# Turning packed probabilities by VectorE blocks and DMAs in place of TensorE transposes

## The chip, the cores and the metric

The kernel runs on one NeuronCore of a Trainium2 chip. Its five engines follow their own instruction queues: TensorE (PE, with its weight loads shown as PEld), VectorE (DVE), ScalarE (ACT), GpSimd (POOL) and SyncE (SP), which here issues nearly all DMAs. The metric is the device time of one execution in microseconds (us), lower is better. The kernel before took 697.37 us, the median of 3 runs (696.98 to 698.82).

## The reference

The inputs are q, k and v of shape 4 x 8 x 768 x 64 (batch, heads, positions, head size) in fp32 and two weight matrices, 512 x 2048 and 2048 x 512. A causal attention with a window of 128 keys and 4 sink keys is followed by a two-layer network:

```
scores = scale * q @ k.T                       # scale = 1/8
keep = (key < 4) | (0 <= query - key < 128)
a = softmax(where(keep, scores, -1e9))
x = (a @ v) with heads side by side            # 3072 tokens x 512
h = x @ w_in
out = max(0.01 * h, h) @ w_out                 # 3072 x 512
```

## The kernel before

The 3072 tokens are cut into 8 **units** of 384 queries (three blocks of 128), two units to a batch element: an even unit holds the first half of a sequence, an odd one the second. In a unit the 8 heads go in 4 **pairs**. Each unit also has 16 steps of the two-layer network (below: **MLP steps**). In an MLP step 12 matmuls form `h` (L584, fp32 split into a high and a low part, so three matmuls per product), ScalarE and VectorE form `g` (L598, L605), ScalarE rounds it to `gh` (L606), GpSimd forms the rest `gl` (L607), and one MLP step later 9 matmuls add into the output `o` (L633); the last three of the nine need `gl`.

The program interleaves the attention of unit u+1 with the MLP of unit u. The order on TensorE is fixed by this interleaving (`manual_schedule` for PE alone): a generator of attention steps is advanced by a table of due steps, eight steps per pair. Work that has to come some score tiles later is put into a list with a lag: `later(LAGT, ...)` with LAGT = 2, and `later(LAGP, ...)` with LAGP = 5 score tiles for the values of a packed pair. The order on the other engines comes from a scheduler.

From the third unit on ("packed" units, 24 pairs, 48 heads) the window of a query block spans the previous and the own key block, and the two halves of the window are stored in one 128 x 128 square: a position of the square holds the own key where it is allowed and the previous block's key elsewhere (`copy_predicated`, L518). So a head has three squares of 128 queries x 128 keys and 4 sink columns, held in `pk` (128 x 396), made by `soft` (L322, L324) and scaled by 1/sum at L525 to L527. The product with the values needs keys on partitions, so each square is turned by a TensorE transpose into a PSUM bank (`turn_packed`, L364), three per head; for the second head of a pair a fourth transpose turns the sinks (`sk`, L366). VectorE then multiplies the turned squares by two triangle masks `low` and `upp` (L383) and writes them side by side into `pt` in SBUF, previous part and own part of each query block; in an even unit the first block needs no mask and is copied by ScalarE (L378). `values` (L406) multiplies `pt` with the values into `acc` (L412 for sinks, L416 for keys), then ScalarE and VectorE split the result into `xh` and `xl` (L432, L433). `pt` has one buffer.

The heads' inputs `qkraw` (three buffers), the pair's values `v` and the pair's sink values `svr` are loaded by SyncE; `svr` lives in the one `rb` buffer.

Of the kernel before, what the change touches and what calls it, by code (L numbers as in the profile page):

```python
# [9 lines left out]
F32 = mybir.dt.float32  # L10
# [10 lines left out]
P = 128  # L21
# [15 lines left out]
NVB = (3, 4)  # L37
SPARE = W3 + NSK
SCALE = 1.0 / D ** 0.5
MASKED = 1.0e38  # L40
# [107 lines left out]
def fast_path(ctx, tc, cpool, qp, qk, vu, vs, vx, vt, wq, out, ident, lims, wz, negm, wmin, wmax):  # L148
# [4 lines left out]
    mpool = ctx.enter_context(tc.tile_pool(name="mpool", bufs=2))  # L153
    iopool = ctx.enter_context(tc.tile_pool(name="iopool", bufs=2))
    psum = ctx.enter_context(tc.tile_pool(name="psum", bufs=1, space=PSUM))
    lim_raw, lim_lo, rest, masks = build_masks(tc, cpool, xpool, lims)
# [89 lines left out]

    def load_sinks(u, pair):
        if native(u):
            sv = apool.tile([SKR, TU], F32, tag="sv", name=f"sv{u}_{pair}")
            if u:  # L250
                nc.sync.dma_start(out=sv[0:T * SKN, :], in_=vx[pair])
            else:
                nc.sync.dma_start(out=sv[0:SKN, :], in_=vs[pair])
            svs[u, pair] = sv
            return
        raw = xpool.tile([SKR, TU], F32, tag="rb", name=f"svr{u}_{pair}", bufs=1)[:, 0:P]
        nc.sync.dma_start(out=raw, in_=vt[u // 2, pair])
        svs[u, pair] = raw

# [39 lines left out]
    def turn_bank(u, name):  # L299
        tags = ("t", "o2") if u == 0 else ("t",)  # L300
        seq["t"] += 1
        return bank(tags[(seq["t"] - 1) % len(tags)], name)
# [56 lines left out]

    def turn_packed(u, pair, o, w, state):  # L360
        half = u % 2
        tp = turn_bank(u, f"t{u}_{pair}_{o}")
        for j in range(T):
            nc.tensor.transpose(out=tp[:, j * P:(j + 1) * P], in_=w[:, j, NSK:], identity=ident)  # L364
        if o:
            nc.tensor.transpose(out=tp[:, TU:], in_=state["sk"].rearrange("p r j h s -> p (r j h s)"), identity=ident)  # L366
            st = xpool.tile([P, P + TU], F32R, tag="r", name=f"st{u}_{pair}")[:, 0:TU]
            state["st"] = st
            nc.vector.tensor_tensor(out=st.rearrange("p (j q) -> p j q", j=T),
                                    in0=tp[:, TU:].rearrange("p (o q) -> p o q", o=1).broadcast_to([P, T, P]),  # L370
                                    in1=late[0][4].rearrange("p (j o) -> p j o", o=1).broadcast_to([P, T, P]),
                                    op=ALU.mult)
        pt = state["pt"][:, o]
        src = tp[:, 0:TU].rearrange("p (j q) -> p j q", j=T)
        if half:
            dst = pt
        else:
            nc.scalar.copy(out=pt[:, 0:P], in_=tp[:, 0:P])  # L378
            dst, src = pt[:, P:5 * P], src[:, 1:T]
        dst = dst.rearrange("p (j t q) -> p t j q", t=2, q=P)  # L380
        n = T - 1 + half
        for t, mask in enumerate(late[0][2:4]):
            nc.vector.tensor_tensor(out=dst[:, t], in0=src,  # L383
                                    in1=mask.rearrange("p (o q) -> p o q", o=1).broadcast_to([P, n, P]), op=ALU.mult)

# [20 lines left out]
    def values(u, pair, state):  # L406
# [7 lines left out]
        for kb, (po, qo, m) in enumerate(parts):  # L414
            for o in range(2):
                nc.tensor.matmul(acc[o * D:(o + 1) * D, qo:qo + m],  # L416
                                 lhsT=vv[:, kb * P + o * D:kb * P + (o + 1) * D],
                                 rhs=state["pt"][:, o, po:po + m], start=kb == 0 and not packed,
                                 stop=packed and kb == len(parts) - 1, skip_group_check=True)
# [22 lines left out]
    def attend(u, pair, pend):  # L442
# [63 lines left out]
        else:  # L506
            for o in range(2):
                h = 2 * pair + o
                sp = split_head(u, h)
                fetch(o)  # L510
                (split_sinks if o else load_sinks)(u, pair)
                w = apool.tile([P, 2 * W3], F32, tag="pk", name=f"pk{u}_{h}", bufs=3)
                w = w[:, 0:T * W1].rearrange("p (j k) -> p j k", j=T)
                sm = apool.tile([P, T], F32, tag="sm", name=f"sm{u}_{h}")
                for j in range(T):
# [8 lines left out]
                    if j == T - 1:  # L524
# [9 lines left out]
                                                op=ALU.subtract)  # L534
                        later(LAGT, lambda o=o, w=w: pt_then(turn_packed, u, pair, o, w, state))
                    yield
        last = u == 0 and pair == NPAIR - 1
        if native(u):
            later(LAGT if last else LAGG, lambda: gather(u, pair, state))
        later(LAGT if last else LAGV if native(u) else LAGP, lambda: values(u, pair, state),  # L540
              "next" if not native(u) else "scores" if u else None)

    def attention_stream():
# [6 lines left out]
        for u in range(NU):  # L550
            for pair in range(NPAIR):
                for _ in attend(u, pair, pend):
                    if pend and pend[0][0] <= count[0] and pend[0][2] == "scores":
                        pend.pop(0)[1]()
                    yield
                    while pend and pend[0][0] <= count[0]:
                        _, f, join = pend.pop(0)
                        f()
                        if not (join == "next" and pend and pend[0][0] <= count[0]):
                            yield  # L560
# [340 lines left out]
```

## Time and profile before

| what | value |
|---|---|
| median of 3 runs | 697.37 us |
| the profiled execution, first to last instruction | 697.4 us |
| TensorE busy | 684.6 us, 98% |
| VectorE busy | 451.0 us, 65% |
| ScalarE, GpSimd busy | 319.4 us, 317.7 us |
| DMA: mean rate | 107 GB/s |
| granted TensorE clock | 0.999 |

Busy time on TensorE counts each matmul until its modelled end, and matmuls overlap, so the share alone does not say how much of the time a removed matmul gives back; start times of neighbouring matmuls do. The page gives no time outside the span of the profiled execution; the span and the median of the runs agree within 0.1 us.

### The profile page before, as it was taken

The numbers are of one execution on the slowest core, as the hardware profiler recorded it, in microseconds if no ns is written. First come the engines' busy times: TensorE is split into PE (matmuls) and PEld (weight loads), VectorE is DVE, ScalarE is ACT, GpSimd is POOL, SyncE is SP. The second block draws the span as 40 slices with busy tenths as digits, with TensorE's granted clock in tenths as the row PEclk, the third lists the DMA queues.
The fourth block names the chain that finished last, engine by engine and source line by source line (L and its number), as shares of the span: only waits on it lengthen the run. The fifth ranks groups of instructions, "written<-read, shape, count | busy, mean of one in ns | idle before, by whom it ended". The sixth has DMA issues, their size and how long they took to land.

```text
span 697.4 us, 11523 instructions
## 1 busy us (share of the span) xinstructions
PE 684.6 (98%) x3938; PEld 596.6 (86%) x3938; DVE 451.0 (65%) x1192; ACT 319.4 (46%) x836; POOL 317.7 (46%) x436
## 2 busy tenths in 40 slices
PE   8999999999999999999999999999999999999996
PEld 5578888898888988888898888898888889899995
DVE  5799999655566665565566565566566666377772
ACT  4867675444444444444444444444444444222221
POOL 3767797544543543443453354344344344112221
PEclk9999999999999999999999999999999999999999
DMA  6657666311213111222113221121221311068761
GB/s 223 214 170 230 212 208 209 128 57 44 73 45 118 47 43 62 61 85 70 59 57 102 70 59 46 62 92 43 69 74 45 118 63 46 1 196 278 257 190 49
DMA packets 30656, 74.55 MB, mean 107 GB/s; under 512 B 3584, under 2 KB 9472, under 8 KB 30592
## 3 DMA queue, kind: packets, MB, share of 16 engines
q1 hardware_dynamic: 30448, 73.63, 32.8%
q8 instruction: 32, 0.52, 0.3%
q14 instruction: 32, 0.26, 0.1%
q10 hardware_dynamic: 144, 0.13, 0.1%
HBM read 67.45 MB, written 6.29 MB: 106 GB/s over the span
## 4 chain that ended last, share of the span: by engine, by line
PE 92%; DVE 2%; DMA 2%; POOL 2%; ACT 1%; issue 1%; SPq 0%; DVEq 0%; POOLq 0%; ACTq 0%
PE h L584 37%; PE o L633 37%; PE acc L416 5%; PE s L315 5%; PE t L364 3%; PE s L310 2%; PE t L351 1%; DMA qkn<-in_qp 1%; DMA qkraw<-in_qk 1%; PE acc L422 0%; PE acc L412 0%; POOL gl L607 0%; ACT pk L324 0%; PE t L366 0%; DMA svr<-in_vt 0%
## 5 line engine op out<-in xcount | busy, mean ns | idle before, releaser
L607 POOL TENSOR_TENSOR gl<-g,gh 128x384 fp32r<-128x384 f32 x121 | 125.0, 1033 | 261.9 <-ACT gh L606 228.4
L584 PE MATMUL h<-xh,wih 128*128 128x384 f32 x512 | 179.1, 350 | 1.1 <-DVE g L605 1.1
L584 PE MATMUL h<-xl,wih 128*128 128x384 f32 x512 | 172.7, 337 | 0.1
L584 PE MATMUL h<-xh,wil 128*128 128x384 f32 x512 | 172.6, 337 | 0.0
L633 PE MATMUL o<-woh,gh 128*128 128x512 f32 (+1 forms) x400 | 153.8, 386 | 0.0
L633 PE MATMUL o<-wol,gh 128*128 128x512 f32 (+1 forms) x400 | 153.2, 386 | 0.0
L324 ACT ACTIVATE pk<-pk,negm 128x132 f32<-128x132 f32 (+1 forms) x192 | 81.6, 425 | 97.6 <-DVE negm L322 97.4
L633 PE MATMUL o<-woh,gl 128*128 128x512 f32 (+1 forms) x400 | 114.7, 388 | 0.7 <-POOL gl L607 0.7
L598 ACT ACTIVATE g<-h 128x384 f32<-128x384 f32 x127 | 62.0, 488 | 112.8 <-PE h L584 96.1
L584 PEld LDWEIGHTS h<-xh,wih 128*128 128x128 f32 x512 | 96.3, 188 | 5.7 <-issue 2.9
L584 PEld LDWEIGHTS h<-xl,wih 128*128 128x128 f32 x512 | 96.6, 189 | 1.6 <-POOL xl L430 0.5
L584 PEld LDWEIGHTS h<-xh,wil 128*128 128x128 f32 x512 | 96.1, 188 | 0.0
L606 ACT CAST gh<-g 128x384 fp32r<-128x384 f32 x128 | 65.7, 513 | 64.3 <-DVE g L605 64.1
L605 DVE TENSOR_TENSOR g<-h,g 128x384 f32<-128x384 f32 x127 | 69.9, 550 | 31.2 <-ACT g L598 30.8
L633 PEld LDWEIGHTS o<-woh,gl 128*128 128x128 f32 x400 | 73.5, 188 | 17.3 <-POOL gl L607 1.6
L633 PEld LDWEIGHTS o<-woh,gh 128*128 128x128 f32 x400 | 75.2, 188 | 10.6
L633 PEld LDWEIGHTS o<-wol,gh 128*128 128x128 f32 x400 | 75.1, 188 | 10.7
L276 POOL TENSOR_TENSOR qksp<-qkraw,qksp 64x396 fp32r<-64x396 f32 (+1 forms) x48 | 56.5, 1177 | 43.4 <-issue 27.5
L518 DVE COPY_PREDICATED s<-tri,s 128x128 f32<-128x128 int8 x120 | 34.9, 291 | 52.0 <-PE s L315 50.5
L315 PEld LDWEIGHTS s<-qksp 128*128 128x128 f32 x288 | 53.4, 188 | 7.9
L275 ACT CAST qksp<-qkraw 128x780 fp32r<-128x780 f32 (+1 forms) x48 | 43.2, 900 | 30.4 <-PE s L315 27.3
L315 PE MATMUL s<-qksp 128*128 128x260 f32 (+1 forms) x288 | 56.3, 277 | 0.0
(123 smaller groups left out, 861.7 us busy)
## 6 DMA issues: line engine op xcount, KB each, us to landing
craw<-in_wq SPq DMA_DIRECT2D x26, 512.0 KB, 4.6
qkraw<-in_qk SPq DMA_DIRECT2D x24, 454.0 KB, 3.2
qkraw<-in_qk SPq DMA_DIRECT2D x24, 390.0 KB, 3.0
wiraw<-in_wq SPq DMA_DIRECT2D x16, 512.0 KB, 3.8
woraw<-in_wq SPq DMA_DIRECT2D x16, 512.0 KB, 3.7
out<-ob SPq DMA_DIRECT2D x23, 256.0 KB, 2.1
v<-in_vu SPq DMA_DIRECT2D x16, 256.0 KB, 2.6
v<-in_vu SPq DMA_DIRECT2D x16, 192.0 KB, 2.5
```

Source lines behind the costliest of these rows:

```text
L275: nc.scalar.copy(out=sp[:, 0:TU + n], in_=raw[:, 0:TU + n])
L276: nc.gpsimd.tensor_tensor(out=sp[D:P, TU:TU + n], in0=raw[D:P, TU:TU + n], in1=sp[D:P, TU:TU + n].bitcast(F32), op=ALU.subtract)
L315: nc.tensor.matmul(pss[0][:, 0:kn], lhsT=sp[:, off + j * P:off + (j + 1) * P], rhs=sp[:, TU + k0:TU + k0 + kn], start=c == 0, stop=c == 1)
L324: nc.scalar.activation(out=w, in_=w, func=AF.Exp, scale=-1.0, bias=neg, accum_out=sm)
L416: nc.tensor.matmul(acc[o * D:(o + 1) * D, qo:qo + m], lhsT=vv[:, kb * P + o * D:kb * P + (o + 1) * D], rhs=state["pt"][:, o, po:po + m], s ...
L518: nc.vector.copy_predicated(out=ps[:, W1:W3], mask=late[0][1], data=ps[:, 0:P])
L584: nc.tensor.matmul(ph[:, 0:TU], lhsT=w[:, cs], rhs=x, start=cc == 0 and c == 0, stop=cc == NCC - 1 and c == 2)
L598: nc.scalar.mul(g, ph[:, 0:TU], 0.01)
L605: anchor[0] = nc.vector.tensor_tensor(out=g, in0=ph[:, 0:TU], in1=g, op=ALU.max)
L606: nc.scalar.copy(out=gh, in_=g)
L607: (nc.vector if u and fc == NFC - 1 else nc.gpsimd).tensor_tensor(out=gl, in0=g, in1=gh.bitcast(F32), op=ALU.subtract)
L633: nc.tensor.matmul(acc, lhsT=(gl if c == 2 else gh)[:, t * P:(t + 1) * P], rhs=(wl if c == 1 else wh)[:, cols], start=f == 0 and c == 0, s ...
```

## The change

In packed units the three TensorE transposes of each head go. In their place `turn_blocks` does this for each head: VectorE transposes all 32 x 32 blocks of the three squares in one instruction (`pk` to `kt`, 128 x 384); one DMA writes `kt` to a DRAM buffer; four DMAs (one for each group of 32 keys) read it back into `pt`, so that the blocks land where a full transpose would have them. The contiguous runs of a read are 96 fp32 numbers (384 bytes). The masking becomes `mask_blocks`: two multiplications from SBUF to SBUF, `pt` by `low` into the second half of `pt` and `pt` by `upp` in place. The columns of `pt` now stand as group of 32 queries, then block, then query, so the matmuls of `values` read their moving operand as runs of 32 columns (`masked_keys`). The sinks' transpose stays on TensorE (`turn_sinks`). `svr` is loaded into the tail of the `pk` tile, and `kt` takes the one `rb` buffer. The first head of a pair is turned at lag 2 and masked at lag 3; the second is turned at lag 0 and masked at lag 2.

```
-        raw = xpool.tile([SKR, TU], F32, tag="rb", name=f"svr{u}_{pair}", bufs=1)[:, 0:P]
-        nc.sync.dma_start(out=raw, in_=vt[u // 2, pair])
-        svs[u, pair] = raw
+        nc.sync.dma_start(out=spare, in_=vt[u // 2, pair])
+        svs[u, pair] = spare
...
-    def turn_packed(u, pair, o, w, state):
...
+    def turn_blocks(u, pair, o, w, state):
+        kt = xpool.tile([P, TU], F32, tag="rb", name=f"kt{u}_{pair}_{o}", bufs=1)
+        nc.vector.transpose(kt.rearrange("p (b j x) -> p b j x", b=NSQ, x=SQ),
+                            w[:, :, NSK:].rearrange("p j (b x) -> p b j x", b=NSQ))
+        far = dpool.tile([P, NSQ, T * SQ], F32, tag="kt", name=f"kd{u}_{pair}_{o}", bufs=2)
+        nc.sync.dma_start(out=far.rearrange("p b x -> p (b x)"), in_=kt)
+        for b in range(NSQ):
+            nc.sync.dma_start(out=state["pt"][b * SQ:(b + 1) * SQ, o, 0:TU].rearrange("c (a x) -> c a x", a=NSQ),
+                              in_=far[:, b].rearrange("(a c) x -> c a x", a=NSQ))
...
+    def mask_blocks(u, o, state):
+        j0 = 1 - u % 2
+        n = T - j0
+        cur, prv = (state["pt"][:, o, i * TU:(i + 1) * TU].rearrange("p (a j x) -> p a j x", a=NSQ, j=T)[:, :, j0:]
+                    for i in range(2))
+        for dst, mask in ((prv, late[0][2]), (cur, late[0][3])):
+            nc.vector.tensor_tensor(out=dst, in0=cur, in1=mask.rearrange("p (a o x) -> p a o x", a=NSQ, o=1)
+                                    .broadcast_to([P, NSQ, n, SQ]), op=ALU.mult)
+
+    def masked_keys(state, o, j0, n):
+        cur = state["pt"][:, o]
+        first = (j0 * SQ, TU + SQ) if j0 >= 0 else (TU, 0)
+        return bass.AP(cur.tensor, cur.offset + first[0],
+                       [cur.ap[0], [first[1], n], [T * SQ, NSQ], [1, SQ]])
...
-                                 rhs=state["pt"][:, o, po:po + m], start=kb == 0 and not packed,
+                                 rhs=masked_keys(state, o, qo // P - (0 if kb or not half else 1), m // P)
+                                 if packed else state["pt"][:, o, po:po + m], start=kb == 0 and not packed,
...
+                w = apool.tile([P, T * W1 + P], F32, tag="pk", name=f"pk{u}_{h}", bufs=3)
...
+                    load_sinks(u, pair, w[:, T * W1:])
...
-                        later(LAGT, lambda o=o, w=w: pt_then(turn_packed, u, pair, o, w, state))
+                        later(0 if o else LAGT, lambda o=o, w=w: pt_then(turn_blocks, u, pair, o, w, state), "quiet")
+                        if o:
+                            later(LAGT, lambda: turn_sinks(u, pair, state))
+                        later(LAGT if o else LAGT + 1, lambda o=o: mask_blocks(u, o, state), "quiet")
```

On VectorE, in the second pair of the sixth unit, the rows from the masks of the pair's first head to the next scaling of a head stood so before:

```order
L268 TENSOR_TENSOR sv_2_4672<-svr_2_4572,sv_2_4672 32x128
L383 TENSOR_TENSOR pt_1_4517<-t_1_0_4518,low 128x3x128
L383 TENSOR_TENSOR pt_1_4517<-t_1_0_4518,upp 128x3x128
L433 TENSOR_TENSOR xl_0_4514<-acc_0_4503,xh_0_4513 128x384
L605 TENSOR_TENSOR g_2_4527<-h_2_4493,g_2_4527 128x384
L518 COPY_PREDICATED s_3_2_4543<-tri,s_3_2_4543 128x128
L322 ISA pk_3_4457,negm<-s_3_2_4543,pm_676 128x132
L322 ISA negm 128x1
L525 TENSOR_SCALAR sm_3_4458<-sm_3_4458 128x3
```

and stand so now (`kt` is the block transpose, `xl_0` belongs to the values of the pair before, `g_1` and `g_2` to two MLP steps that follow each other):

```order
L364 STREAM_TRANSPOSE kt_1_0_4607<-pk_2_4428 128x384
L623 TENSOR_TENSOR g_1_4563<-h_1_4544,g_1_4563 128x384
L270 TENSOR_TENSOR sv_2_4760<-pk_4_4663,sv_2_4760 32x128
L445 TENSOR_TENSOR xl_0_4593<-acc_0_4582,xh_0_4592 128x384
L533 COPY_PREDICATED s_3_2_4615<-tri,s_3_2_4615 128x128
L324 ISA pk_3_4533,negm<-s_3_2_4615,pm_678 128x132
L324 ISA negm 128x1
L623 TENSOR_TENSOR g_2_4629<-h_2_4596,g_2_4629 128x384
L388 TENSOR_TENSOR pt_1_4606<-pt_1_4606,low 128x384
L540 TENSOR_SCALAR sm_3_4537<-sm_3_4537 128x3
L388 TENSOR_TENSOR pt_1_4606<-pt_1_4606,upp 128x384
```

The masks moved from ahead of `xl_0` to behind `g_2`, the next MLP step's `g`, and the block transpose stands one MLP step ahead of them.

On SyncE, for the same pair, the queue held three loads and no store of probabilities before:

```order
L244 DMA qkraw_4_4452<-in_qk 128x908
L244 DMA qkraw_5_4570<-in_qk 128x908
L257 DMA svr_2_4572<-in_vt 128x128
L234 DMA v_1_4127<-in_vu 128x512
L244 DMA qkraw_6_4670<-in_qk 128x908
```

and holds these now (`kd` is the DRAM buffer):

```order
L259 DMA pk_4_4663<-in_vt 128x128
L367 DMA kd_1_0_4609<-kt_1_0_4607 128x384
L237 DMA v_2_4424<-in_vu 128x512
L369 DMA pt_1_4606<-kd_1_0_4609 32x4x96 x4
L247 DMA qkraw_0_4980<-in_qk 128x780
L367 DMA kd_1_1_4649<-kt_1_1_4647 128x384
L369 DMA pt_1_4606<-kd_1_1_4649 32x4x96 x4
```

Between two loads of heads there are now one write and four reads, in order behind each other; the loads `qkraw` and `v` stand between them.

## Rows read from the trace of the kernel before

**Rows 1.** Page, busy us of each engine, share of the span, instructions.
```profile
PE 684.6 (98%) x3938; PEld 596.6 (86%) x3938; DVE 451.0 (65%) x1192; ACT 319.4 (46%) x836; POOL 317.7 (46%) x436
```
**Rows 2.** Busy time by stretches (stretch, its length, each engine's busy us).
```profile
107.00:190.00 83.00, 80.92 (x462) 71.29 (x461) 54.07 (x146) 39.64 (x109) 44.50 (x54) 1.00 0.31 101
...
358.00:441.00 83.00, 83.00 (x479) 73.67 (x478) 52.35 (x145) 37.77 (x98) 36.63 (x47) 1.00 0.22 66
```
**Rows 3.** Page, the chain that ended last, by engine and by line.
```profile
PE 92%; DVE 2%; DMA 2%; POOL 2%; ACT 1%; issue 1%; SPq 0%; DVEq 0%; POOLq 0%; ACTq 0%
PE h L584 37%; PE o L633 37%; PE acc L416 5%; PE s L315 5%; PE t L364 3%; PE s L310 2%; PE t L351 1%; DMA qkn<-in_qp 1%; DMA qkraw<-in_qk 1%; PE acc L422 0%; PE acc L412 0%; POOL gl L607 0%; ACT pk L324 0%; PE t L366 0%; DMA svr<-in_vt 0%
```
**Rows 4.** Groups by shape, transposes: busy us, mean ns | idle before.
```profile
L364 PE MATMUL t<-ident,pk 128*128 128x128 f32 x144 | 24.8, 281 | 0.0
```
**Rows 5.** Timeline of PE, an even unit (start us, us, engine, instruction).
```profile
136.34 1.30 PE L416 MATMUL acc<-pt,v 128*64 128x256 f32 x12
137.57 0.55 PE L364 MATMUL t<-ident,pk 128*128 128x128 f32 x3
137.88 0.48 PE L633 MATMUL o<-woh,gh 128*128 128x512 f32 x1
138.19 0.39 PE L633 MATMUL o<-wol,gh 128*128 128x512 f32 x1
138.42 0.39 PE L633 MATMUL o<-woh,gh 128*128 128x512 f32 x1
...
147.72 0.49 PE L364 MATMUL t<-ident,pk 128*128 128x128 f32 x3
148.04 0.27 PE L366 MATMUL t<-ident,sk 128*128 128x128 f32 x1
```
**Rows 6.** Timeline of PE, values of an odd unit.
```profile
387.23 1.52 PE L416 MATMUL acc<-pt,v 128*64 128x128 f32 x16
```
**Rows 7.** Groups by shape on DVE: busy us, mean ns | idle before.
```profile
L383 DVE TENSOR_TENSOR pt<-t,low 128x384 f32<-128x384 f32 x24 | 13.3, 553 | 16.9 <-PE t L364 16.9
L383 DVE TENSOR_TENSOR pt<-t,low 128x256 f32<-128x256 f32 x24 | 10.0, 416 | 1.3 <-ACT pt L378 1.3
...
L607 DVE TENSOR_TENSOR gl<-g,gh 128x384 fp32r<-128x384 f32 x7 | 3.9, 557 | 3.5 <-ACT gh L606 3.5
```
**Rows 8.** Lines L527 and L525: duration ns min/median/max, first and last start.
```profile
L527 DVE TENSOR_TENSOR pk<-pk,sm x48: 560/1182/1390, 109.8 to 600.0; 128x396 f32<-128x396 f32 x48
...
L525 DVE TENSOR_SCALAR sm<-sm x48: 157/763/1054, 108.0 to 599.5; 128x3 f32<-128x3 f32 x48
```
**Rows 9.** DMA issues: count, KB each, median us to landing.
```profile
out<-ob SPq DMA_DIRECT2D x23, 256.0 KB, 2.1
...
svr<-in_vt SPq DMA_DIRECT2D x24, 64.0 KB, 1.8
...
sv<-in_vs SPq DMA_DIRECT2D x4, 48.0 KB, 4.0
```
**Rows 10.** Timeline of SP's queue, three DMAs issued in a row.
```profile
380.64 1.52 SPq L648 DMA_DIRECT2D out<-ob  x3
```
**Rows 11.** Timeline of all engines, from one MLP step's `h` to the use of `gl`.
```profile
333.46 0.47 ACT L598 ACTIVATE g<-h 128x384 f32<-128x384 f32 x1
...
333.99 0.55 DVE L605 TENSOR_TENSOR g<-h,g 128x384 f32<-128x384 f32 x1
...
334.56 0.51 ACT L606 CAST gh<-g 128x384 fp32r<-128x384 f32 x1 [0.63 <-DVE g L605]
...
334.94 0.34 PE L584 MATMUL h<-xh,wih 128*128 128x384 f32 x1
...
335.12 0.34 PE L584 MATMUL h<-xl,wih 128*128 128x384 f32 x1
...
335.15 1.01 POOL L607 TENSOR_TENSOR gl<-g,gh 128x384 fp32r<-128x384 f32 x1 [0.46 <-PE s L315]
...
338.89 0.86 PE L633 MATMUL o<-woh,gl 128*128 128x512 f32 x3
```

More of the change, by code (lines that the diff above doesn't have):

```diff
@@ L38 @@
 SPARE = W3 + NSK
+SQ = 32
+NSQ = P // SQ
 SCALE = 1.0 / D ** 0.5
@@ L154, in fast_path @@
     iopool = ctx.enter_context(tc.tile_pool(name="iopool", bufs=2))
+    dpool = ctx.enter_context(tc.tile_pool(name="dpool", bufs=1, space=bass.MemoryType.DRAM))
     psum = ctx.enter_context(tc.tile_pool(name="psum", bufs=1, space=PSUM))
@@ L245, in load_head, with load_sinks @@
         raws[u, h] = raw
-    def load_sinks(u, pair):
+    def load_sinks(u, pair, spare=None):
         if native(u):
@@ L358, in turn_native @@
             split_sinks(u, pair)
-    def turn_packed(u, pair, o, w, state):
[L361 to L384, printed above, removed]
@@ new lines, in turn_sinks @@
+    def turn_sinks(u, pair, state):
+        tp = turn_bank(u, f"t{u}_{pair}")
+        nc.tensor.transpose(out=tp[:, 0:P], in_=state["sk"].rearrange("p r j h s -> p (r j h s)"), identity=ident)
+        st = xpool.tile([P, P + TU], F32R, tag="r", name=f"st{u}_{pair}")[:, 0:TU]
+        state["st"] = st
+        nc.vector.tensor_tensor(out=st.rearrange("p (j q) -> p j q", j=T),
+                                in0=tp[:, 0:P].rearrange("p (o q) -> p o q", o=1).broadcast_to([P, T, P]),
+                                in1=late[0][4].rearrange("p (j o) -> p j o", o=1).broadcast_to([P, T, P]),
+                                op=ALU.mult)
@@ L510, in attend @@
                 fetch(o)
-                (split_sinks if o else load_sinks)(u, pair)
-                w = apool.tile([P, 2 * W3], F32, tag="pk", name=f"pk{u}_{h}", bufs=3)
+                w = apool.tile([P, T * W1 + P], F32, tag="pk", name=f"pk{u}_{h}", bufs=3)
+                if o:
+                    split_sinks(u, pair)
+                else:
+                    load_sinks(u, pair, w[:, T * W1:])
                 w = w[:, 0:T * W1].rearrange("p (j k) -> p j k", j=T)
@@ L534, in attend @@
                                                 op=ALU.subtract)
-                        later(LAGT, lambda o=o, w=w: pt_then(turn_packed, u, pair, o, w, state))
+                        later(0 if o else LAGT, lambda o=o, w=w: pt_then(turn_blocks, u, pair, o, w, state), "quiet")
+                        if o:
+                            later(LAGT, lambda: turn_sinks(u, pair, state))
+                        later(LAGT if o else LAGT + 1, lambda o=o: mask_blocks(u, o, state), "quiet")
                     yield
@@ L540, in attend @@
         later(LAGT if last else LAGV if native(u) else LAGP, lambda: values(u, pair, state),
-              "next" if not native(u) else "scores" if u else None)
+              "scores" if u and native(u) else None)
     def attention_stream():
@@ L558, in attention_stream @@
                         f()
-                        if not (join == "next" and pend and pend[0][0] <= count[0]):
+                        if join != "quiet":
                             yield
```

## The prediction

> **What bounds the kernel now.** I read the page's busy line first, then stretches of one unit each, then the chain of waits, then start times on TensorE. The reader is to see that TensorE is busy 98% of the span [rows 1] and, in a middle unit, all of it: 83.00 of 83.00 us [rows 2]; no other engine reaches two thirds. The chain that ended last runs through TensorE for 92% of the span, and the transposes that go have 3% of it [rows 3]. So in the stretch this change touches (some 110 to 600 us, from the first and last start in rows 8) TensorE has no slack to lose, and what leaves its queue comes off the span, unless a wait appears in its place. The profiled execution (697.4 us) and the median (697.37) agree, so no correction is made between them.
>
> **What is removed.** 48 heads times 3 transposes are 144 matmuls. Their group is busy 24.8 us [rows 4], but that counts each run of three to its modelled end, 0.49 to 0.55 us. Starts tell what they occupy: three transposes start at 137.57, and the next matmul at 137.88, 0.31 us later; at 147.72 the next starts at 148.04, 0.32 us later [rows 5]. 48 x 0.32 = 15.4 us. After the first run the next interval is 0.31 (137.88 to 138.19) where 0.23 is usual (138.19 to 138.42), so up to 0.08 more could go, 48 x 0.08 = 3.8 us; but it may belong to any change between small and large matmuls, and one stays, so I count none of it. Ends of this term: 15.4 and 24.8; I take 15.4, since starts and not ends decide when the next matmul goes. The sinks' transpose stays and changes nothing. ScalarE loses the copy of an even unit's first block; it is off the chain [rows 3], so nothing.
>
> **What is added on TensorE.** Nothing in number: `values` has the same matmuls and columns, so no gain is possible. But the moving operand is now read in runs of 32 columns. No row shows such a read. The lower bound is no cost; the upper I set at twice the time: an even pair's 12 matmuls take 1.30 us [rows 5], an odd pair's 16 take 1.52 [rows 6], so 12 x 1.30 + 12 x 1.52 = 33.8 us. I take zero: matmuls here keep the pace of their columns, and a run is still 32 numbers side by side. Rival three keeps the other end.
>
> **What is added on VectorE.** 48 block transposes of 128 x 384. Not shown before; the nearest row of equal width from SBUF to SBUF is the `gl` that VectorE forms, 0.557 us, and the nearest that is slow is the scaling of a head, 128 x 396, with a median of 1.182 us [rows 7, 8]; a 256-column mask bounds it from below at 0.416. I take 0.56: 27 us over the kernel. The masks stay 96 instructions of the same widths (0.553 and 0.416 from PSUM), but now have two SBUF sources. Price between 0.557, the quick row, and 1.182, the slow one, for 384 columns. The scaling takes 0.560 at best and 1.390 at worst for the same shape, and an addition on 3 numbers 0.157 to 1.054 [rows 8]: some VectorE instructions wait about one GpSimd instruction (1.01 us, rows 11) when the two meet. I take half of the way, 0.3 us more for each mask, 29 us. VectorE then has 451 + 27 + 29 = 507 us of about 683, 74%. Per pair of a middle unit it is idle (83.00 - 52.35) / 4 = 7.7 us [rows 2] and gets 2 x 0.56 + 4 x 0.3 = 2.3 us more (4.8 at the dear end, 2 x 1.18 + 4 x 0.62). Cover is there in sum; what matters is the queue behind. Behind masks and transpose waits `g`, behind it `gh`, `gl`, and TensorE's last three `o` matmuls. That chain has `gl` ready at 335.15 + 1.01 = 336.16 and used at 338.89 [rows 11]: 2.7 us of slack per MLP step. The second head's transpose (0.56) and the first head's two masks (2 x 0.86 in place of 2 x 0.55) add 1.2 us ahead of one `g`: hidden.
> The Trainium skill has a rule for this (SBUF — State Buffer, "SBUF: two separate sides"): VectorE and GpSimd share one port pair as an exclusive lock, which a VectorE instruction with two SBUF inputs and a GpSimd instruction that reads SBUF take in turn, each for its whole length. It agrees with the spread of rows 8 and speaks against this change, since it gives every new mask that wait, and it works the other way round on `gl`. By that rule alone the time would be that of the first rival.
>
> **What is added on SyncE and DMA.** Five DMAs per head, 240 in all, in one queue with the loads. Three issued in a row take 1.52 us [rows 10], so 0.51 each, 5.1 us per pair of about 20. For the first head of a pair the order matters: its reads write into the single `pt`, so they wait until the `values` of the pair before are through on TensorE (call that T). The write to DRAM was issued one MLP step earlier and has landed (2.1 us for 256 KB, rows 9). The last of four reads is issued at T + 1.5 and lands 1.8 us later if it is like `svr` (64 KB), 4.0 if like `sv` (48 KB, the size of a read, among the first loads) [rows 9]: T + 3.3 or T + 5.5. I take 3.3, since `svr` is a row of the same stretch. VectorE wants them behind the next `g`: 12 `h` and 2 score matmuls at 0.18 us (334.94 to 335.12), then 0.47 and 0.55 us [rows 11], T + 3.6 with a hand-over. So no wait, by 0.3 us only; at 5.5 the masks are 1.9 us late. For the second head the block transpose stands right behind the scaling; write and reads need about 2.1 + 3.3 = 5.4 us, and its masks come one and a half MLP steps (some 7 us) later, with the values five score tiles behind the head; hidden. The loads `qkraw` wait behind these DMAs, but have two spare buffers, so some 20 us; `svr` and `v` are needed a head later. DMA engines are busy 0.22 of a middle unit [rows 2]; 48 heads x 0.39 MB fit.
> The Trainium skill (DMA: Bandwidth & Descriptors, "Specifications") asks for at least 512 bytes per transfer for full rate; a read here moves runs of 384. `svr` has runs of 512, so no row shows shorter ones, and the rule weighs on the second rival.
>
> **Sum.** 697.4 - 15.4 = 682.0. In the third unit TensorE already waited 83.00 - 80.92 = 2.1 us, while VectorE was fullest, 54.07 [rows 2]; more VectorE work there, and loads that stand in the queue at the end of attention, I put at 1 us (an estimate, half of that idle time). **683 us**, 2.1% faster; own range 673 (all 24.8 us given back) to 690.
>
> **Rivals.**
> 1. *VectorE gives half back.* Masks and transposes meet GpSimd each time, 1.18 us each: ahead of a `g` 3 x 1.18 - 2 x 0.55 = 2.4 us more, and `gl` held once by 1.18, 3.6 against 2.7 of slack. 0.9 us per pair in half of the 24 pairs is 11 us: **693**. For it: rows 8. Against: it needs meetings at each instruction, and GpSimd is busy 46% [rows 1].
> 2. *Slower: the first head's blocks come late.* Reads land at T + 5.5, the masks block VectorE 1.9 us, and with the 2.4 us above `gl` is 1.9 + 2.4 - 2.7 = 1.6 us late in each pair: 24 x 1.6 = 38 us, **720**. It decides from 15.4 / 24 = 0.64 us of TensorE wait per pair on. For it: the margin of 0.3 us and the 4.0 us row. Against: DMA load is light there, and both dear ends must meet.
> 3. *Slower: the runs of 32 halve the pace of `values`.* 682 + 33.8 = **716**; break-even at 1.46 times. For it: no row shows such an operand. Against: as above.
> 4. *The transposes' place was free.* If weight loads set TensorE's pace, other matmuls would stretch: **697**. Against: the starts around the runs return to 0.23 us at once [rows 5].
>
> **How the numbers follow.** Forecast 0.70, rival 1 0.14, rival 2 0.09, rival 3 0.05, rival 4 0.02. About 0.3% is what a measurement of this kernel can tell from no change, so faster means under 695.3 and slower over 699.5. Faster: 0.70 and most of rival 1 (0.08): 0.78. Same: rival 4 and a part of rival 1: 0.06. Slower: rivals 2, 3 and the tail of rival 1: 0.16. The range reaches from 673 to 699: below 673 lies nearly nothing, above 699 about 0.16.
>
> **What would show it.** TensorE's matmul count down by 144; where a run of three transposes stood, a start interval shorter by 0.32 us; a pair's period down from about 20.7 by 0.6 us. `values` in 1.30 and 1.52 us as before (else rival 3). On VectorE block transposes near 0.56 us; masks between 0.56 and 1.18, and no wait for the DMA into `pt` longer than some tenths of a us (else rival 2). TensorE still over 97% busy in a middle unit; if it waits for `gl` or `g` there, rival 1 or 2. The forecast is wrong if a middle unit takes 83 us or more.

## The result, and the profile after

The changed kernel took 702.53 us (median of 6 runs, 700.35 to 706.56) against 697.84 us (696.98 to 698.95) for the kernel before on the same chip: ratio 1.007, 95% interval 1.0046 to 1.0095, so 0.7% slower where 2.1% faster was forecast. The profiled execution spans 701.1 us.

The page after, against [rows 1] and [rows 3] (busy us of each engine; then the chain that ended last by engine and by line; `h` is now L602, `g` L623, `gh` L624, `gl` L625, `o` L651, the block transpose L364, the write to DRAM L367, the four reads L369, the masks L388):

```profile
PE 679.6 (97%) x3794; PEld 584.4 (83%) x3794; DVE 478.3 (68%) x1240; ACT 306.9 (44%) x812; POOL 327.1 (47%) x436
...
PE 65%; DVE 13%; DMA 12%; SPq 4%; issue 2%; ACT 2%; POOL 0%; DVEq 0%; POOLq 0%
```

TensorE has 144 matmuls fewer, as it should, and 5 us less busy time, but the chain went from 92% TensorE to 65%: a quarter of it now runs through VectorE and the DMAs. Two unit stretches, against [rows 2]:

```profile
107.00:190.00 83.00, 76.75 (x414) 66.70 (x413) 55.56 (x144) 36.27 (x96) 43.27 (x51) 0.96 0.42 127
358.00:441.00 83.00, 80.18 (x442) 69.53 (x441) 53.70 (x146) 33.79 (x92) 38.64 (x45) 0.98 0.34 99
```

TensorE stood idle 6.3 and 2.8 us there (2.1 and 0 before), and the granted clock fell under 1. The engine it waits for is not full: VectorE was busy 53.7 of 83 us. So it is a wait, not a load. The list of waits names it (who waited for whom: us in total, times, longest), here the kernel before, then the changed one:

```profile
ACT gh L606 <- DVE g L605: 64.1, 94, 2.4
```

```profile
ACT gh L624 <- DVE g L623: 87.4, 86, 5.3
DVE pt L388 <- DMA pt<-kd: 66.6, 40, 4.6
PEld o L651 <- ACT gh L624: 9.4, 15, 2.7
PE o L651 <- ACT gh L624: 4.6, 4, 2.4
```

VectorE stood 66.6 us before masks whose blocks had not landed, 1.7 us each time. The prediction said some tenths. Of the 66.6 us, 53.9 belong to second heads (all 24) and 12.8 to first heads (16 of 24). TensorE's weight loads for `o` waited for `gh` 15 times, its matmuls 4 times; the list of the kernel before has no such wait.

Where it hurts is seen at the start of the sixth unit (here and in the next three fences: start us, duration, engine, instruction, and in brackets the idle time and what ended it). Second head of the first pair, on VectorE:

```profile
375.83 0.57 DVE L364 STREAM_TRANSPOSE kt<-pk 128x384 f32<-128x384 f32 x1
...
376.85 0.56 DVE L623 TENSOR_TENSOR g<-h,g 128x384 f32<-128x384 f32 x1
...
384.32 0.56 DVE L388 TENSOR_TENSOR pt<-pt,low 128x384 f32<-128x384 f32 x1 [4.22 <-DMA pt<-kd]
384.79 0.69 DVE L665 COPY ob<-o 128x512 f32<-128x512 f32 x1
385.39 0.55 DVE L388 TENSOR_TENSOR pt<-pt,upp 128x384 f32<-128x384 f32 x1
385.86 0.55 DVE L623 TENSOR_TENSOR g<-h,g 128x384 f32<-128x384 f32 x1
```

its DMAs on SyncE's queue:

```profile
373.93 0.35 SPq L247 DMA_DIRECT2D qkraw<-in_qk  x1
376.43 0.34 SPq L367 DMA_DIRECT2D kd<-kt  x1
380.79 1.74 SPq L369 DMA_DIRECT2D pt<-kd  x4
```

and what followed on ScalarE and TensorE:

```profile
386.45 0.51 ACT L624 CAST gh<-g 128x384 fp32r<-128x384 f32 x1 [5.26 <-DVE g L623]
```

```profile
387.01 0.50 PE L651 MATMUL o<-woh,gh 128*128 128x512 f32 x1 [2.39 <-ACT gh L624]
...
390.35 2.20 PE L427 MATMUL acc<-pt,v 128*64 128x128 f32 x16
```

Read it backwards: TensorE's `o` waits 2.39 us for `gh`, `gh` for `g`, and `g` stands on VectorE behind two masks that wait 4.22 us for reads, which waited 4.36 us (376.43 to 380.79) for the write. TensorE did not need those masks before the values of the pair, at 389.89. It needed the `g` that was queued behind them. After the wait the clock fell too: the 16 matmuls took 2.20 us, not 1.52 as in [rows 6], and this is the granted clock (third number from the end) of that stretch:

```profile
388.00:392.00 4.00, 4.00 (x19) 2.62 (x19) 2.33 (x9) 2.18 (x7) 1.47 (x4) 0.57 0.72 268
```

That is the lower of its two levels (1.2 of 2.4 GHz) for most of 4 us. In most pairs the wait is milder. In the first pair of the fourth unit the block transpose starts at 213.63, VectorE is at the masks 3.8 us later (217.42) and stands 2.01 us until the blocks are there at 219.43; `o` then lacks 0.89 us:

```profile
219.43 1.26 DVE L388 TENSOR_TENSOR pt<-pt,low 128x384 f32<-128x384 f32 x1 [2.01 <-DMA pt<-kd]
...
221.68 0.55 DVE L623 TENSOR_TENSOR g<-h,g 128x384 f32<-128x384 f32 x1
...
222.82 0.50 PE L651 MATMUL o<-woh,gh 128*128 128x512 f32 x1 [0.89 <-ACT gh L624]
```

The prices taken for single operations, against [rows 7] (busy us, mean ns | idle before) and [rows 9] (count, KB, median us to landing):

```profile
L364 DVE STREAM_TRANSPOSE kt<-pk 128x384 f32<-128x384 f32 x48 | 27.5, 572 | 0.5
L388 DVE TENSOR_TENSOR pt<-pt,low 128x384 f32<-128x384 f32 x24 | 18.7, 780 | 30.7 <-DMA pt<-kd 30.5
L388 DVE TENSOR_TENSOR pt<-pt,upp 128x256 f32<-128x256 f32 x24 | 18.3, 763 | 0.2
L388 DVE TENSOR_TENSOR pt<-pt,upp 128x384 f32<-128x384 f32 x24 | 16.1, 673 | 0.2
L388 DVE TENSOR_TENSOR pt<-pt,low 128x256 f32<-128x256 f32 x24 | 15.5, 644 | 36.2 <-DMA pt<-kd 36.1
```

```profile
kd<-kt SPq DMA_DIRECT2D x48, 192.0 KB, 1.9
pt<-kd SPq DMA_DIRECT2D x192, 48.0 KB, 2.0
```

and the values with their new operand, an even and an odd unit, as long as in [rows 5] and [rows 6]:

```profile
139.93 1.30 PE L427 MATMUL acc<-pt,v 128*64 128x256 f32 x12
...
225.28 1.52 PE L427 MATMUL acc<-pt,v 128*64 128x128 f32 x16
```

### The profile page after: what moved, and what is told of

The parts are those of the page before. It is cut to its first block, busy times and chain, and to the rows that moved or that the text cites. A ratio compares the mean times of both kernels' runs of the same rounds, so it can differ in the third digit from the quotient of the medians.

```text
span 701.1 us, 11730 instructions
## 1 busy us (share of the span) xinstructions
PE 679.6 (97%) x3794; PEld 584.4 (83%) x3794; DVE 478.3 (68%) x1240; ACT 306.9 (44%) x812; POOL 327.1 (47%) x436
## 4 chain that ended last, share of the span: by engine, by line
PE 65%; DVE 13%; DMA 12%; SPq 4%; issue 2%; ACT 2%; POOL 0%; DVEq 0%; POOLq 0%
PE o L651 27%; PE h L602 25%; DMA pt<-kd 7%; PE acc L427 5%; DMA kd<-kt 5%; DVE pt L388 4%; SPq L369 4%; PE s L317 3%; PE s L312 2%; PE t L353 1%; DVE sm L540 1%; DVE g L623 1%; DVE kt L364 1%; DVE pk L542 1%; DVE pk L324 1%
## 5 line engine op out<-in xcount | busy, mean ns | idle before, releaser
L625 POOL TENSOR_TENSOR gl<-g,gh 128x384 fp32r<-128x384 f32 x121 | 130.4, 1077 | 181.3 <-ACT gh L624 176.3
L602 PE MATMUL h<-xh,wih 128*128 128x384 f32 x512 | 180.8, 353 | 3.9 <-DVE g L623 3.9
L602 PE MATMUL h<-xl,wih 128*128 128x384 f32 x512 | 173.5, 339 | 0.1
L602 PE MATMUL h<-xh,wil 128*128 128x384 f32 x512 | 173.4, 339 | 0.0
L651 PE MATMUL o<-woh,gh 128*128 128x512 f32 (+1 forms) x400 | 156.1, 392 | 5.0 <-ACT gh L624 4.6
L651 PE MATMUL o<-wol,gh 128*128 128x512 f32 (+1 forms) x400 | 153.4, 387 | 0.0
L651 PE MATMUL o<-woh,gl 128*128 128x512 f32 (+1 forms) x400 | 115.3, 390 | 0.3 <-POOL gl L625 0.3
L602 PEld LDWEIGHTS h<-xh,wih 128*128 128x128 f32 x512 | 96.7, 189 | 14.8 <-issue 6.5
L624 ACT CAST gh<-g 128x384 fp32r<-128x384 f32 x128 | 65.7, 513 | 87.7 <-DVE g L623 87.4
L602 PEld LDWEIGHTS h<-xl,wih 128*128 128x128 f32 x512 | 96.9, 189 | 1.5 <-POOL xl L442 0.4
L602 PEld LDWEIGHTS h<-xh,wil 128*128 128x128 f32 x512 | 96.6, 189 | 0.0
L623 DVE TENSOR_TENSOR g<-h,g 128x384 f32<-128x384 f32 x127 | 70.1, 552 | 35.9 <-ACT g L616 35.6
L651 PEld LDWEIGHTS o<-woh,gh 128*128 128x128 f32 x400 | 75.5, 189 | 21.0 <-ACT gh L624 9.4
L651 PEld LDWEIGHTS o<-woh,gl 128*128 128x128 f32 x400 | 74.1, 189 | 16.8 <-POOL gl L625 0.7
L651 PEld LDWEIGHTS o<-wol,gh 128*128 128x128 f32 x400 | 75.5, 189 | 10.7
L388 DVE TENSOR_TENSOR pt<-pt,low 128x256 f32<-128x256 f32 (+1 forms) x48 | 34.2, 712 | 66.9 <-DMA pt<-kd 66.6
L277 ACT CAST qksp<-qkraw 128x780 fp32r<-128x780 f32 (+1 forms) x48 | 43.1, 899 | 66.6 <-PE s L317 57.7
```

Of the source, the lines that this page charges most:

```text
L277: nc.scalar.copy(out=sp[:, 0:TU + n], in_=raw[:, 0:TU + n])
L388: nc.vector.tensor_tensor(out=dst, in0=cur, in1=mask.rearrange("p (a o x) -> p a o x", a=NSQ, o=1) .broadcast_to([P, NSQ, n, SQ]), op=ALU. ...
L602: nc.tensor.matmul(ph[:, 0:TU], lhsT=w[:, cs], rhs=x, start=cc == 0 and c == 0, stop=cc == NCC - 1 and c == 2)
L623: anchor[0] = nc.vector.tensor_tensor(out=g, in0=ph[:, 0:TU], in1=g, op=ALU.max)
L624: nc.scalar.copy(out=gh, in_=g)
L625: (nc.vector if u and fc == NFC - 1 else nc.gpsimd).tensor_tensor(out=gl, in0=g, in1=gh.bitcast(F32), op=ALU.subtract)
```

## The experiments

Ratios are against the kernel before, run on the same chip; its medians there lie between 697.7 and 698.3 us. Several verdicts rest on **periods**: the time from the first matmul of one pair's values to that of the next, read from TensorE's timeline of each profiled execution. "First" is the pair that ends with the first packed values, "odd" and "even" the medians of the four periods that begin in the fourth unit and of the three that stay in the fifth (with their range where it is over 0.2), "sixth" the two pairs around the place shown above.

| kernel | median us | ratio, 95% interval | first | odd | even | sixth |
|---|---|---|---|---|---|---|
| before | 697.84 | 1 | 25.76 | 20.72 | 20.46 | 20.43, 20.73 |
| after | 702.53 | 1.0070 (1.0046 to 1.0095) | 30.02 | 20.50 (20.26 to 20.53) | 19.94 | 23.25, 21.74 |
| e1_mask_later | 701.18 | 1.0044 (1.0026 to 1.0061) | 29.50 | 20.46 (20.14 to 20.54) | 19.93 | 20.39, 21.74 |
| e2_no_dma | 687.85 | 0.9851 (0.9834 to 0.9867) | 26.79 | 20.18 | 19.83 | 19.90, 20.19 |
| e3_first_only | 696.90 | 0.9981 (0.9972 to 0.9990) | 28.23 | 20.51 | 20.22 | 20.24, 20.53 |
| e4_second_only | 699.54 | 1.0017 (1.0007 to 1.0027) | 27.30 | 20.66 (20.47 to 20.95) | 20.21 | 20.52, 20.80 |
| e7_behind_g | 691.56 | 0.9909 (0.9894 to 0.9923) | 27.81 | 20.18 | 19.83 | 20.25, 20.66 |
| e8_behind_more | 690.74 | 0.9898 (0.9880 to 0.9915) | 27.26 | 20.18 | 19.84 | 19.90, 20.19 |
| e5_no_turn | 685.25 | 0.9812 (0.9795 to 0.9829) | 28.69 | 20.12 | 19.82 | 19.83, 20.11 |
| e6_reads_twice | 691.17 | 0.9895 (0.9873 to 0.9917) | 27.71 | 20.18 | 19.84 | 20.04, 20.27 |
| e10_twice_in_front | 704.57 | 1.0088 (1.0060 to 1.0117) | 27.68 | 20.31 (20.13 to 20.81) | 20.35 (19.95 to 20.37) | 20.88, 21.97 |
| e9_best | 687.47 | 0.9840 (0.9819 to 0.9860) | 26.78 | 20.18 | 19.84 | 19.90, 20.19 |

**e1_mask_later.** One lag more for the second head's masks.

```
-   later(LAGT if o else LAGT + 1, lambda o=o: mask_blocks(u, o, state), "quiet")
+   later(LAGT + 1, lambda o=o: mask_blocks(u, o, state), "quiet")
```

> The changed kernel with one number different: the second head's two masks are issued three lags after its turn, as the first head's are, not two. Theory A (VectorE comes to the second head's masks some 2 us before the write and the four reads have landed, 5.8 us after the block transposition was asked for, and g, gh and TensorE's o stand behind them): VectorE's 66.6 us of waiting on the pt reads falls to under 25 us, the waits of gh on g fall well below 87 us, and the time is about 692 us (688 to 696). Rival B (the new masks and transpositions slow VectorE and GpSimd by their load alone): the time stays within 2 us of the changed kernel, 702.5 us. Rival C (the removed transposes give back less than 15.4 us): TensorE's waits go, but the time stays at or above 697 us.

Measured 701.2 us, and VectorE still waits 64.8 us on the reads. By its numbers this looks like theory A failing. It was the experiment that failed: the lag does not set VectorE's order, which comes from a scheduler. In the traces every engine has the same instructions in the same order as in the changed kernel, so e1 is that kernel run once more. It tells nothing for or against A, but it shows what the lag does not control, and how executions of one program differ: the write at the place shown above, issued at 376.43 here too, let its reads go after 2.04 us (378.47) and not 4.36, and that pair took 20.39 us, not 23.25.

**e2_no_dma.** The block transposition writes into `pt`; no write, no reads.

```
-   kt = xpool.tile([P, TU], F32, tag="rb", name=f"kt{u}_{pair}_{o}", bufs=1)
-   nc.vector.transpose(kt.rearrange(...), w[:, :, NSK:].rearrange(...))
+   nc.vector.transpose(state["pt"][:, o, 0:TU].rearrange(...), w[:, :, NSK:].rearrange(...))
-   far = dpool.tile(...)
-   nc.sync.dma_start(...)            # and the four reads
```

> The changed kernel without the movement of the blocks between partitions: the block transposition writes its result straight into pt, and the write to DRAM and the four reads are left out, so the output is not the reference's. VectorE, ScalarE, GpSimd and TensorE have the same instructions as in the changed kernel. Theory A: no wait for the DMAs is left, a steady pair of units costs what its gain of some 0.25 to 0.55 us says or less, and the time is 682 to 689 us. Rival B (load or contention on VectorE and GpSimd): 698 us or more, because the instructions on these engines are the same. Rival C (the transposes give back less): 690 to 697 us with TensorE without waits.

687.85 us, 14.7 us below the changed kernel, with the same instructions on VectorE, ScalarE, GpSimd and TensorE. So the amount of new work on VectorE is not the loss; what e2 lacks is the movement. Two things differ besides. The meetings with GpSimd are rarer: counting a mask as slowed over 0.45 us (256 columns) or 0.60 us (384), 7 of 96 are slowed here and 45 in the changed kernel, so that e2 leaves this half of rival B open; e7 below, with 38 slowed and 691.6 us, and e10, with 15 and 704.6 us, close it. And VectorE's order differs, so e2 does not tell late blocks from their place in the queue; e7 does. In the middle units TensorE is back at full time:

```profile
358.00:441.00 83.00, 83.00 (x467) 73.22 (x466) 55.97 (x157) 37.42 (x102) 41.81 (x50) 1.00 0.23 71
```

**e3_first_only and e4_second_only.** Blocks and DMAs for one head of each pair, TensorE for the other.

```
+   if o == 0:                        # e4: if o == 1
        later(0 if o else LAGT, lambda o=o, w=w: pt_then(turn_blocks, u, pair, o, w, state), "quiet")
        ...
+   else:
+       later(LAGT, lambda o=o, w=w: pt_then(turn_packed, u, pair, o, w, state), None if o else "quiet")
```

> Only the first head of each pair is turned by VectorE and the DMAs; the second head is turned by TensorE, as in the kernel before. Theory A (the loss sits in the second head's chain): faster than the kernel before by about half of the 15.4 us, 690 us (687 to 694). Rival B (load): about half way between the two kernels, 700 us. Rival D (the first head's blocks are late): slower than 698 us.

> Only the second head of each pair is turned by VectorE and the DMAs; the first head is turned by TensorE, as in the kernel before. Theory A: it carries the loss of the changed kernel with half of its gain, 700 to 708 us, with VectorE waiting some 50 to 65 us for the pt reads in total. Rival B (load): about half way between the two kernels, 700 us, with the waits on the reads small. Rival D (the first head's blocks are late): faster than the kernel before, about 690 us.

The signs are as theory A had them: the first head alone is 0.2% faster than before with 7.3 us of waiting on the reads, the second alone 0.2% slower with 45.6 us. The time of e4, just under the 700 to 708 of theory A, would also be rival B's 700; its waits, and e2, speak against B. The size of e3 missed: 690 was expected, 697 came. Its usual pair gains 0.21 to 0.24 us where one head's transposes were put at 0.32, and its first packed pair loses 2.5 us. Why one run of three gives back less while the other stays was not settled. Rival D (the first head late) falls.

**e7_behind_g.** An edge on VectorE puts the second head's masks behind the `g` that was traced last.

```
+    def mask_behind(u, o, state):
+        with tc.issue_after(anchor[0].ins):          # anchor[0]: the last g
+            mask_blocks(u, o, state)
-   later(LAGT if o else LAGT + 1, lambda o=o: mask_blocks(u, o, state), "quiet")
+   later(3 if o else LAGT + 1, lambda o=o: mask_behind(u, o, state), "quiet")
```

VectorE's order for a second head (third pair of the sixth unit), the changed kernel first, then e7:

```
L623 TENSOR_TENSOR g_7_4914<-h_7_4895,g_7_4914 128x384
L377 TENSOR_TENSOR st_2_4932<-t_2_4930,own 128x384
...
L388 TENSOR_TENSOR pt_2_4829<-pt_2_4829,low 128x384
L388 TENSOR_TENSOR pt_2_4829<-pt_2_4829,upp 128x384
L623 TENSOR_TENSOR g_8_4960<-h_8_4934,g_8_4960 128x384
L540 TENSOR_SCALAR sm_6_4888<-sm_6_4888 128x3
```

```
L627 TENSOR_TENSOR g_7_4914<-h_7_4895,g_7_4914 128x384
L377 TENSOR_TENSOR st_2_4932<-t_2_4930,own 128x384
...
L627 TENSOR_TENSOR g_8_4958<-h_8_4934,g_8_4958 128x384
L388 TENSOR_TENSOR pt_2_4829<-pt_2_4829,low 128x384
L544 TENSOR_SCALAR sm_6_4888<-sm_6_4888 128x3
L388 TENSOR_TENSOR pt_2_4829<-pt_2_4829,upp 128x384
```

> The changed kernel with one ordering edge more: the second head's two masks are issued three lags after its turn and held on VectorE behind the g that was traced last, so that in VectorE's order they stand behind the g that they stood in front of. The DMAs are the same. Theory A2 (the movement by DMAs costs nothing but the place of the masks: g, and with it gh and TensorE's o, stand behind two masks that wait for the reads): TensorE's waits for gh nearly go, a steady pair costs 19.9 and 20.2 us as without the DMAs (e2), and the time is 690 us (688 to 694), what is left above e2 being the first packed pair. Rival E (the write, the reads and their traffic themselves slow the loads or other engines, wherever the masks stand): within 2 us of the changed kernel, 700 us or more.

691.56 us: 11 us gained by exchanging places. TensorE and GpSimd have the same instructions in the same order, and the other engines and the DMAs the same instructions; on VectorE the second head's masks and `g` change places (the first head's masks get the edge too and stay where they were), and three activations on ScalarE and six loads on SyncE stand elsewhere. The usual periods are those of e2, so rival E (traffic) falls. The place shown above, in e7 (`g` is L627 here):

```profile
370.63 0.57 DVE L364 STREAM_TRANSPOSE kt<-pk 128x384 f32<-128x384 f32 x1
...
376.08 0.55 DVE L627 TENSOR_TENSOR g<-h,g 128x384 f32<-128x384 f32 x1
377.86 1.26 DVE L388 TENSOR_TENSOR pt<-pt,low 128x384 f32<-128x384 f32 x1 [1.24 <-DMA pt<-kd]
```

VectorE still waits for the blocks, but `g` has gone ahead, and VectorE has the time. In the next pair e7 even has a wait of 3.40 us (masks at 400.11, behind a write whose last rows ended 3.8 us after its issue): TensorE then waits 0.33 us before the values, and the pair takes 20.66 us, 0.47 more than in e2. In the changed kernel 4.22 us in front of `g` cost 3.35 us (23.25 against 19.90).

**e8_behind_more.** As e7, with `later(4 if o ...)`, so behind the next head's scaling.

> As e7_behind_g, with the second head's masks one score tile later still (four lags), behind the scaling of the next head's probabilities in VectorE's order. Theory A2: VectorE's waiting on the pt reads falls from 66.6 us to under 15 us, and the time is the same as e7_behind_g's or up to 3 us less, 688 to 691 us; if the masks now end too late for the values (five lags), TensorE waits there and the time is above e7_behind_g's. Rival E: 700 us or more.

690.74 us; its runs (689.3 to 691.7) overlap those of e7 (691.0 to 692.5). VectorE's wait is nearly gone, and TensorE gains little more by it (us in total, times, longest; of 32.8 us in e7):

```profile
DVE pt L388 <- DMA pt<-kd: 13.4, 13, 4.4
```

So VectorE's wait as such is cheap; what stands behind it is not.

**e5_no_turn.** The kernel before without its transposes.

```
-        for j in range(T):
-            nc.tensor.transpose(out=tp[:, j * P:(j + 1) * P], in_=w[:, j, NSK:], identity=ident)
-        src = tp[:, 0:TU].rearrange("p (j q) -> p j q", j=T)
+        src = w[:, :, NSK:]
```

> The kernel before without the 144 transposes of probabilities on TensorE from the third unit on: the masks read the unturned squares, so the output is not the reference's. It measures what these transposes cost by themselves. My sum: 15.4 us less than before, 682 to 684 us. By the sum of their own durations: 24.8 us less, 673 us. If their place was mostly free or what follows them is late anyway: 690 us or more. From e2 (688 us, with VectorE's block transpositions and masks in place): 10 us less than before, 687 to 688 us.

685.25 us, 12.4 us less than the kernel before on the same chip. The usual pair gains 0.60 and 0.64 us, 0.30 to 0.32 per head: the term of the sum. Over 24 pairs that is 15 us, of which the first packed pair takes 2.9 back.

**e6_reads_twice.** The changed kernel with eight reads per head.

```
-        for b in range(NSQ):
+        for b in [*range(NSQ), *range(NSQ)]:
```

> The changed kernel with each of the four reads of a head's blocks issued twice, eight in all: the chain from the block transposition to the last block becomes some 1.8 us longer (four issues on SyncE at 0.44 us each). Theory A2: TensorE loses these 1.8 us, or most of them, for each second head wherever VectorE already waits, in some 16 of 24 pairs: 715 to 735 us. Rival E (traffic): the extra 48 reads of 4 x 48 KB move the time in proportion to the traffic that was added, by about 4 x 192/384 = 2 us, to 704 to 706 us. If VectorE's wait costs TensorE nothing: 702 us.

691.17 us: faster by 11 us for more traffic and a longer chain, which no theory had. VectorE's order offers a reason: the scheduler now put the second head's masks behind `g`, as the edge in e7 does (third pair of the sixth unit: `L623 g_8`, then `sm`, its reciprocal, then the masks); it also moved the first head's masks, behind the second head's block transposition. Whether it is the place of `g` was tried next.

**e10_twice_in_front.** e6 with `g` held behind the first of the second head's masks.

```
+                    with tc.issue_after((masked[0] or anchor[0]).ins):   # masked[0]: the low mask, second head
                         anchor[0] = nc.vector.tensor_tensor(out=g, in0=ph[:, 0:TU], in1=g, op=ALU.max)
```

> e6_reads_twice with one ordering edge more: each g of the third unit's time and after is held on VectorE behind the first of the second head's two masks that was traced last. The DMAs are those of e6_reads_twice, eight reads per head; in e6 VectorE's order has the second head's masks behind g, here g stands behind the first mask again, as in the changed kernel. Theory A2 (the order of mask and g on VectorE is what costs): TensorE waits for gh in nearly every pair, by the changed kernel's wait and the 1.8 us more that the four extra reads take, 1 to 2.5 us for each of 24 pairs, and the time is 715 to 750 us, 24 to 60 us above e6's 691.2 us. Rival E (something else in e6 made it fast, such as other DMA times): within 5 us of e6.

704.57 us, 13.4 us above e6 with the same DMAs and the same order on TensorE: the order on VectorE alone turns 1% faster into 1% slower. `o` waits for `gh` again, which it does not in e6:

```profile
PE o L655 <- ACT gh L628: 7.7, 11, 2.3
```

The size was overrated (24 to 60 us expected): TensorE's matmuls wait for `gh` 11 times, not in each of 24 pairs.

**e9_best.** e8, with the first packed pair and the second head of the last pair left to TensorE.

```
+    def by_tensor(u, pair, o):
+        return (u, pair) == (2, 0) or (u, pair, o) == (NU - 1, NPAIR - 1, 1)
...
+   if by_tensor(u, pair, o):
+       later(LAGT, lambda o=o, w=w: pt_then(turn_packed, u, pair, o, w, state), None if o else "quiet")
```

> e8_behind_more with two places given back to TensorE: both heads of the first packed pair (third unit) and the second head of the last pair are turned by TensorE as in the kernel before; all others by VectorE and DMAs, with the second head's masks held behind g. In e8 the first packed pair took 27.26 us against 25.76 before, with a 2.4 us wait for GpSimd's sk and a granted clock of 0.66 for 5 us behind it, and the last pair's values waited 0.8 us for their masks. Theory F (in the first packed pair VectorE and GpSimd set the pace, so TensorE's removed work is no gain there and the clock falls behind the wait): the first pair goes back to some 26 us, the last wait goes, and the time is 688.5 us (687.5 to 689.7). Rival: the two places cost what they cost in e8 for another reason: 690 to 692 us.

687.47 us, the fastest of all: 1.6% below the kernel before, 2.1% below the changed one. Theory F holds in part only: the first packed pair went from 27.26 to 26.78 us, not to 26. There TensorE still waits for GpSimd's `sk` (the waits of e8, then of e9, between 110 and 140 us):

```profile
PE t L374 <- POOL sk L552: 2.4, 1, 2.4
PE h L606 <- DVE g L627: 2.3, 2, 1.6
```

```profile
PE t L376 <- POOL sk L577: 1.8, 1, 1.8
PE h L634 <- DVE g L655: 0.8, 2, 0.5
```

The 0.8 us wait of the last pair's values for their masks is gone. The rest of e9's gain over e8 (2.0 us in the profiled executions) lies at the end too, where TensorE's order of the pieces changed as well (the last period is 12.51 against 14.79 us, the stretch behind it 92.4 against 91.6), so how much of it is that wait was not separated.

## Why the prediction was wrong

**The step that failed** is the second head's cover: "write and reads need about 2.1 + 3.3 = 5.4 us, and its masks come one and a half MLP steps (some 7 us) later ... hidden". The DMAs were sized well: in the fourth unit 5.2 us from the end of the transposition (213.63 + 0.58) to the masks (219.43). The cover was not: between the transposition and the masks VectorE's order has one `g`, not one and a half steps, and VectorE arrives 3.8 us after the transposition starts; it then waits, in all 24 pairs. And the step asked only whether the blocks are in time for the values. It did not name, as the prediction did for the first head, what is queued behind the waiting masks: the next `g`, on which TensorE's `o` hangs. The 2.7 us of slack [rows 11] belong to `gl`, which the last three of nine matmuls need. `gh`, which the first six need, has 2.4 us: ready at 334.56 + 0.51 = 335.07, first used at 337.50 in the same trace. In the fourth unit the wait (2.01), the masks and an output copy held `g` for 4.3 us (217.42 to 221.68). e7, and e6 against e10, show that this place alone is worth 11 to 13 us. The prediction gives its range two upper ends, 690 under the sum and 699 under the numbers; the time lies above both. Of the 19.5 us between 683 and 702.5, 14.7 go with the movement (down to e2's 687.9), which is this step; the other 5 are sizes, named below.

**Where the time went.** By the starts of the values in the profiled executions, the changed kernel loses 13.8 us to e2 between the last values of the second unit and the last of all: 3.2 in the first packed pair, 4.9 around the sixth unit's start, 1.2 each at the fourth's and eighth's, and the rest in small pieces. Against that stand 10.7 us that e2 gains on the kernel before. The 4.9 us hang on a write of 4.36 us; in e8 and in e1 the same write behind the same load took 2.04 us, so such a delay is not in every execution, and e1's profiled one, without it at this place, still spans 699.5 us. The trace has a likely cause: of the write's 128 rows 120 are moved by 377.94; the other eight follow from 379.43 on, as a packet of 16 KB in a queue of the kind "instruction" ends (378.51 to 379.44). e1 has no such packet at its 376.43; in e7 five writes end over 2.8 us after their issue, each with such a packet beside it. The trace does not say which of the 16 DMA engines took what, so that the packet held these rows is inferred from the times. The wider spread of the changed kernel's runs (6.2 us against 2.0) fits it.

**Right.** 0.32 us per head for its three transposes (e5: 0.30 to 0.32); runs of 32 columns at no cost (1.30 and 1.52 us), so rival 3 falls; the block transpose at 0.56 us (0.572); the reads, in runs of 384 bytes, land after 2.0 us where 1.8 was taken. Rival 2, as it was put, falls with e3, where the first head alone is 0.2% faster. "No wait" for the first head was wrong by a little: 16 of 24 wait, 0.8 us on average, 2.8 at most, but their masks stand behind `g` already. The rival's mechanism was right, a late read holding VectorE in front of what TensorE needs, but in the other head and on `gh`. Masks were put at 0.85 and 0.72 us and took 0.64 to 0.78. Rival 1 falls: e7 has all of VectorE's new work and nearly as many slowed masks (38 against 45), and its usual periods are still those of e2. VectorE's load was put at 507 us and came to 478.3: the masks took 68.6 us in place of 46.3, but the scaling of the heads 37.5 in place of 52.2, so the meetings with GpSimd in part only moved. The rule that it rests on (the Trainium skill, SBUF — State Buffer, "SBUF: two separate sides") agrees with masks of 256 columns that take 0.41 us at best and 1.42 at worst: all 45 slowed masks begin while a GpSimd instruction is under way. It did not decide the time. Rival 4 falls with e5.

**Mis-sized.** With no block late at all (e2) the change gives some 10 us, not 14: the usual pair gains 0.54 to 0.63 us, near the 0.64 of the sum, but the ends do not. One term is the 1 us for the third unit: its first packed pair loses 1.0 us without DMAs (e2), 2.9 in e5, 4.3 in the changed kernel. TensorE waits there for `g` and `sk` in all of these and in the kernel before (1.1 and 1.0 us), so removed matmuls are no gain, and behind such a wait the clock goes down (0.66 in e8 from 125 to 130 us):

```profile
125.00:130.00 5.00, 3.29 (x11) 3.30 (x12) 1.49 (x3) 0.00 (x0) 1.57 (x3) 0.66 0.45 136
```

The last period is 1.0 us longer in e2 than before (14.79 against 13.78), but TensorE's order of the pieces changed there, so how much of it is a loss stays open. No run reached the forecast of 683 us: e2 comes to 687.9 without moving anything, e9 to 687.5 with all of the computation.

## What to carry to other kernels

When an in-order engine gets an instruction that waits for a DMA, read what its queue holds behind that instruction, not only when its result is needed: here the masks were done 4 us before the values needed them (385.94 to 389.89), and `g`, their neighbour, came 2.4 us too late. Where a scheduler writes that queue, take the place of each instruction from the written order, and pin it with an edge; a lag in the program, or a change that looks like pure cost (e6), moves it or not in ways that the source does not tell. And time an offload on the chain it creates (transposition, write, landing, four issues, landing), not on the operations' own times.

## What the runs showed of the hardware that was not expected

- The same write of 192 KB, 2.5 us behind the same load of 454 KB, took 4.36 us in one execution and 2.04 in two others; the median is 1.9. In the slow one eight of its 128 rows were moved only when a 16 KB packet of the kind "instruction" had ended.
- A TensorE wait costs more than itself: behind 2.39 us of wait the clock was granted at 0.57 for 4 us, and 16 matmuls took 2.20 in place of 1.52 us.
- VectorE's block transpose of 128 x 384 fp32 took 559 to 580 ns in all 48 cases, 14 of them begun while a GpSimd instruction was under way, while masks of the same width, with two SBUF inputs, spread from 0.54 to 1.35 us.
